# Feature-major attention on 64x64 array tiles, with softmax sums from ones matmuls, in a fused attention and FFN kernel

## The chip, the cores and the metric

The kernel runs on one core of one Trainium2 chip. The metric is device time in microseconds (us), the lower the better.

## The reference, cut to what matters

Linformer attention, then an FFN with a squared relu. There are 8 batches of 8 heads, 1024 tokens and 64 features per head. The keys and values are first projected from 1024 tokens to 64 rows.

```python
k_proj = einsum('ks,bhsd->bhkd', E, k)          # E: 64 x 1024
v_proj = einsum('ks,bhsd->bhkd', F, v)
scores = q @ k_proj.T / sqrt(64)                # per head 1024 x 64
attn   = softmax(scores)
x      = attn @ v_proj                          # heads side by side: 8192 x 512
out    = maximum(x @ w_in, 0)**2 @ w_out        # 512 -> 2048 -> 512
```

All matmuls run in bf16. Per batch the FFN needs 2 x 128 matmuls of 128x128 weights and 512 columns.

## The kernel before

The code is written so that the attention of batch b+1 stands ahead of the FFN of batch b; a scheduler then fills the waits of the one with matmuls of the other. The parts that the change touches:

```python
# per pair of heads: Q transposed, scores on block-diagonal K, softmax
for i in range(NI):
    nc.tensor.transpose(ps_qt[:, i, :], Q_sb[:, i, h0*D:(h0+2)*D], ident_bf[:, :])
nc.vector.tensor_copy(QT_sb[:], ps_qt ...)
for ch in range(2):
    nc.tensor.matmul(ps_sc, lhsT=kprojT_blk[:, pr, :], rhs=QT_sb[:, ch*512:(ch+1)*512], ...)
    nc.scalar.activation(expT_sb[...], ps_sc[:], AF.Exp, scale=SCALE)
# values: tokens on the partitions; two more columns of vprojB give the sums
for (i0, ng) in [(0, 3), (3, 3), (6, 2)]:
    for gi in range(ng):
        nc.tensor.matmul(ps_av[:, gi, :], lhsT=expT_sb[:, i*P:(i+1)*P], rhs=vprojB[:, pr, :], ...)
    nc.vector.reciprocal(recip, ps_av[..., 2*D:2*D+2])
    nc.vector.tensor_tensor(out=x_b..., in0=ps_av..., in1=recip..., op=ALU.mult)
...
# x is token-major, the FFN wants it feature-major: 32 transposes per batch
for cb in range(NCB):
    for i in range(NI):
        nc.tensor.transpose(ps_xt[:, i, :], x_b[:, i, cb*P:(cb+1)*P], ident_bf[:, :])
    nc.scalar.copy(xT_b[:, cb, :], ps_xt ...)
```

The loads stand in this order on one queue: K, V, Q of batch 0, w_in, w_out, then K, V, Q of batch 1 and so on.

The softmax here doesn't subtract the row's maximum and nothing guards it: scores larger than these inputs give would overflow.

## Time and profile before

| | before |
|---|---|
| time, median of 4 runs | 581.15 us (580.04 to 582.84) |
| span of the profiled execution | 577.8 us |
| TensorE (PE) busy | 92% |
| one steady batch | 65.86 us |
| first FFN matmul | 57.81 us |

From the page of the kernel before, the busy time by engine, and the share of the DMA engines' time in 40 slices of 14.4 us (tenths, 9 is 90% or more):

```profile
PE 533.3 (92%) x2998; PEld 259.8 (45%) x3056; DVE 180.9 (31%) x412; ACT 242.9 (42%) x353; POOL 45.7 (8%) x32
DMA  9999999038901792028901694010010101010101
```

TensorE is the bound, and in the first seven slices the DMA engines are busy for 90% or more. The windows view of the kernel before, one batch of the steady part (start:end, length, busy time and instructions of each engine, granted clock, DMA share, GB/s):

```profile
189.50:255.40 65.90, 65.22 (x376) 31.83 (x382) 21.89 (x51) 30.15 (x45) 5.30 (x3) 1.00 0.54 81
```

TensorE is busy for 65.2 of 65.9 us at full clock. What fills a batch is read from the timeline of TensorE in the kernel before (start, length, engine, line, what, count); first the prologue, then a steady batch:

```profile
48.75 0.58 PE L111 MATMUL ps_bank<-K_sb,ET_sb 128*64 128x512 bf16 x1 [5.97 <-DMA K_sb<-in_k_dram]
53.85 0.64 PE L119 MATMUL ps_bank<-V_sb,FT_sb 128*64 128x512 bf16 x1 [4.52 <-DMA V_sb<-in_v_dram]
...
57.81 0.96 PE L229 MATMUL ps_h<-xT_b,w_in_sb 128*128 128x512 bf16 x3 [0.33 <-issue]
...
60.50 0.62 PE L163 MATMUL ps_bank<-ident_bf,Q_sb 128*128 128x128 bf16 x8 [1.50 <-DMA Q_sb<-in_q_dram]
...
190.76 0.38 PE L111 MATMUL ps_bank<-K_sb,ET_sb 128*64 128x512 bf16 x1
190.77 0.38 PE L119 MATMUL ps_bank<-V_sb,FT_sb 128*64 128x512 bf16 x1
191.08 1.04 PE L229 MATMUL ps_h<-xT_b,w_in_sb 128*128 128x512 bf16 x3
...
193.74 0.59 PE L175 MATMUL ps_bank<-QT_sb,kprojT_blk 128*128 128x512 bf16 x2
194.17 1.46 PE L229 MATMUL ps_h<-xT_b,w_in_sb 128*128 128x512 bf16 x6
195.46 0.78 PE L191 MATMUL ps_bank<-vprojB,expT_sb 128*128 128x130 bf16 x8
196.08 0.61 PE L163 MATMUL ps_bank<-ident_bf,Q_sb 128*128 128x128 bf16 x8
196.53 1.67 PE L229 MATMUL ps_h<-xT_b,w_in_sb 128*128 128x512 bf16 x7
...
210.32 3.40 PE L229 MATMUL ps_h<-xT_b,w_in_sb 128*128 128x512 bf16 x15
```

How to read it. A length of a group runs to the end of its last matmul, and one matmul lasts 0.38 us, but they overlap in the pipe. The cost of a matmul is therefore the distance between starts: (3.40 - 0.38) / 14 = 0.216 us for 512 columns. So a batch's 256 FFN matmuls take 55.3 us, and the other 10.6 us of a period are the attention of the next batch. One pair of heads takes 0.43 us for its scores (193.74 to 194.17), 0.62 to 0.73 us for its values (0.62 from 195.46 to 196.08) and 0.45 us for its Q transposes (196.08 to 196.53). The last K and V matmuls of the projection start 0.01 us apart on two 64-column halves of the array and share one slot. Their slot would end at 190.77 + 0.216 = 190.99 us, but the next matmul on the full array starts at 191.08 us: 0.1 us is lost in the change of tiling.

The prologue is another matter. TensorE waits 5.97 us for batch 1's K and 4.52 us for its V, and only then starts its first FFN matmul, at 57.81 us. It is also slower there: the granted clock was 0.62 between 22.0 and 57.8 us, against 1.00 in the steady batch, and the slots of batch 1's projection last 0.43 us, not 0.216.

### The profile page before, as it was taken

What the parts mean: (1) busy time and instruction counts of PE and PEld (TensorE: products, weight loads), DVE (VectorE), ACT (ScalarE), POOL (GpSimd) and SP (SyncE); (2) the same over time, 40 slices, a digit from 0 to 9 for tenths busy, and PEclk for the clock granted to TensorE, in tenths of its full rate; (3) what the DMA queues carried; (4) which work ended last, traced back from release to release, by engine and by line L of the source; (5) the groups of instructions that cost most, each with busy time, mean ns of one, the idle gap of its engine ahead of it and who ended that gap; (6) DMA issues with size and microseconds to landing.
All of it is one profiled execution on the core that took longest, in us unless ns stands there. A gap on an engine that the chain in (4) does not pass through costs nothing.

```text
span 577.8 us, 7241 instructions
## 1 busy us (share of the span) xinstructions
PE 533.3 (92%) x2998; PEld 259.8 (45%) x3056; DVE 180.9 (31%) x412; ACT 242.9 (42%) x353; POOL 45.7 (8%) x32
## 2 busy tenths in 40 slices
PE   0662899999999999999999999999999999999997
PEld 0340454445444454445544454445544454444443
DVE  3350550217121550317221460307312360303030
ACT  0131562436442572526543571526533472515251
POOL 7300320012000120012000120000000000000000
PEclk9865999999999999999999999999999999999999
DMA  9999999038901792028901694010010101010101
GB/s 163 190 207 189 193 192 142 19 76 130 105 36 49 133 110 75 1 77 142 110 36 38 122 115 84 8 74 1 20 54 31 42 2 56 18 56 19 74 0 74
DMA packets 94305, 47.13 MB, mean 82 GB/s; under 512 B 67008, under 2 KB 85440, under 8 KB 94272
## 3 DMA queue, kind: packets, MB, share of 16 engines
q0 software_dynamic: 84896, 29.36, 45.0%
q10 hardware_dynamic: 9376, 17.31, 7.8%
q8 instruction: 24, 0.39, 0.3%
q14 instruction: 9, 0.07, 0.0%
HBM read 59.24 MB, written 16.78 MB: 132 GB/s over the span
## 4 chain that ended last, share of the span: by engine, by line
PE 78%; DMA 6%; DVE 5%; ACT 4%; issue 4%; POOL 2%; ACTq 0%; POOLq 0%
PE ps_bank L246 38%; PE ps_h L229 31%; DMA Q_sb<-in_q_dram 6%; ACT expT_sb L182 3%; PE ps_bank L214 2%; PE ps_bank L191 2%; PE ps_bank L111 2%; PE ps_bank L163 2%; DVE hsqT L239 2%; ACT h_relu L237 1%; DVE x_b L201 1%; DVE QT_sb L169 1%; PE ps_bank L175 1%; DVE recip L199 1%; POOL Q_sb L78 1%
## 5 line engine op out<-in xcount | busy, mean ns | idle before, releaser
L229 PE MATMUL ps_h<-xT_b,w_in_sb 128*128 128x512 bf16 x990 | 231.6, 379 | 1.9 <-issue 0.3
L246 PE MATMUL ps_bank<-w_out_sb,hsqT 128*128 128x512 bf16 x1000 | 222.2, 379 | 1.3
L237 ACT ACTIVATE h_relu<-ps_h 128x1024 bf16<-128x1024 f32 x128 | 130.8, 1031 | 81.0 <-PE ps_h L229 81.0
L239 DVE TENSOR_TENSOR hsqT<-h_relu 128x1024 bf16<-128x1024 bf16 x128 | 88.5, 691 | 232.8 <-ACT h_relu L237 232.8
L246 PEld LDWEIGHTS <-hsqT 128*128 128x128 bf16 x1024 | 100.1, 98 | 120.9
L229 PEld LDWEIGHTS <-w_in_sb 128*128 128x128 bf16 x1024 | 98.0, 98 | 112.1 <-issue 3.8
L254 ACT COPY o_sb<-ps_bank 128x512 f32<-128x512 f32 x64 | 37.5, 587 | 174.6 <-PE ps_bank L246 174.6
L182 ACT ACTIVATE expT_sb<-ps_bank 128x512 bf16<-128x512 f32 x64 | 34.7, 596 | 27.9 <-PE ps_bank L175 27.9
L201 DVE TENSOR_TENSOR x_b<-ps_bank,recip 128x384 bf16<-128x384 f32 (+1 forms) x96 | 44.5, 491 | 0.2
L129 DVE CAST kproj_sb<-ps_bank 64x512 bf16<-64x512 f32 x8 | 5.5, 683 | 102.0 <-PE ps_bank L119 83.5
L78 POOL DMA_DIRECT2D Q_sb<-in_q_dram x8 | 28.5, 3564 | 103.1 <-PE ps_bank L163 46.2
L215 ACT COPY xT_b<-ps_bank 128x1024 bf16<-128x1024 bf16 x32 | 30.8, 1031 | 7.5 <-PE ps_bank L214 7.5
L191 PE MATMUL ps_bank<-vprojB,expT_sb 128*128 128x130 bf16 x256 | 26.4, 230 | 3.4 <-ACT expT_sb L182 1.4
L199 DVE RECIPROCAL recip<-ps_bank 128x6 f32<-128x6 f32 (+1 forms) x96 | 18.1, 189 | 24.5 <-PE ps_bank L191 23.7
L191 PEld LDWEIGHTS <-expT_sb 128*128 128x128 bf16 x256 | 15.8, 101 | 21.1 <-ACT expT_sb L182 20.6
L163 PE MATMUL ps_bank<-ident_bf,Q_sb 128*128 128x128 bf16 x256 | 21.3, 231 | 4.0 <-DMA Q_sb<-in_q_dram 4.0
L68 POOL DMA_DIRECT2D K_sb<-in_k_dram x8 | 9.5, 1188 | 191.0 <-PE ps_bank L119 190.2
L111 PE MATMUL ps_bank<-K_sb,ET_sb 128*64 128x512 bf16 x64 | 19.1, 444 | 6.0 <-DMA K_sb<-in_k_dram 6.0
L175 PE MATMUL ps_bank<-QT_sb,kprojT_blk 128*128 128x512 bf16 x64 | 20.3, 400 | 4.1 <-DVE QT_sb L169 4.1
L119 PE MATMUL ps_bank<-V_sb,FT_sb 128*64 128x512 bf16 x64 | 18.7, 444 | 4.7 <-DMA V_sb<-in_v_dram 4.7
L169 DVE COPY QT_sb<-ps_bank 128x1024 bf16<-128x1024 bf16 x32 | 21.4, 670 | 4.6 <-PE ps_bank L163 4.4
L137 ACT CAST vprojB<-ps_bank 64x64 bf16<-64x64 f32 x32 | 6.7, 209 | 32.4 <-PE ps_bank L119 32.1
(31 smaller groups left out, 116.0 us busy)
## 6 DMA issues: line engine op xcount, KB each, us to landing
out_dram<-o_sb ACTq DMA_DIRECT2D x64, 256.0 KB, 2.0
K_sb<-in_k_dram POOLq DMA_DIRECT2D x8, 1024.0 KB, 9.5
V_sb<-in_v_dram POOLq DMA_DIRECT2D x8, 1024.0 KB, 14.5
Q_sb<-in_q_dram POOLq DMA_DIRECT2D x8, 1024.0 KB, 15.1
w_in_sb<-in_moe_w_in_dram POOLq DMA_DIRECT2D x1, 2048.0 KB, 27.5
w_out_sb<-in_moe_w_out_dram POOLq DMA_DIRECT2D x1, 2048.0 KB, 35.9
e_f_108<-in_E_dram ACTq DMA_DIRECT2D x1, 256.0 KB, 3.5
e_f_122<-in_F_dram ACTq DMA_DIRECT2D x1, 256.0 KB, 7.1
```

Source lines behind the costliest of these rows:

```text
L78: nc.gpsimd.dma_start(Q_sb[:].rearrange("p i (h d) -> p i h d", h=H), q[b].rearrange("h (p i) d -> p i h d", i=NI),)
L111: nc.tensor.matmul(ps_k[0:KP, :], lhsT=ET_sb[:, i, :], rhs=K_view[:, :, i, :], start=(i == 0), stop=(i == NI - 1), tile_position=(0, 0),)
L163: nc.tensor.transpose(ps_qt[:, i, :], Q_sb[:, i, h0 * D:(h0 + 2) * D], ident_bf[:, :],)
L182: nc.scalar.activation(expT_sb[:, ch * CHW:(ch + 1) * CHW], ps_sc[:], AF.Exp, scale=SCALE)
L191: nc.tensor.matmul(ps_av[:, gi, :], lhsT=expT_sb[:, i * P:(i + 1) * P], rhs=vprojB[:, pr, :], start=True, stop=True,)
L201: nc.vector.tensor_tensor(out=out_view.rearrange("p g (h d) -> p g h d", h=2), in0=ps_av[:, 0:ng, 0:2 * D].rearrange("p g (h d) -> p g h d ...
L215: nc.scalar.copy(xT_b[:, cb, :], ps_xt[:].rearrange("p i q -> p (i q)"))
L229: nc.tensor.matmul(ps_h[:, half, :], lhsT=w_in_sb[:, cb, fb * P:(fb + 1) * P], rhs=xT_b[:, cb, ch * TCH:(ch + 1) * TCH], start=(cb == 0), ...
L237: nc.scalar.activation(h_relu[:], ps_h[:].rearrange("p a t -> p (a t)"), AF.Relu)
L239: nc.vector.tensor_tensor(out=hsq_view, in0=h_relu[:], in1=h_relu[:], op=ALU.mult)
L246: nc.tensor.matmul(ps_o[:, :], lhsT=hsqT[:, fb, tb * P:(tb + 1) * P], rhs=w_out_sb[:, fb, :], start=(fb == 0), stop=(fb == NFB - 1),)
L254: nc.scalar.copy(o_sb[:], ps_o[:])
```

## The change

The intent is to take work off TensorE. Attention now works with features on the partitions throughout, so its output is already what the FFN wants, and the 32 x transposes per batch go. The price is that softmax sums can no longer be a column of the values matmul. A matmul of ones with the exponentials puts each token's sum on all 64 partitions of its head. 1/sum is Exp(-Ln(sum)) on ScalarE, and one multiply of 128x1024 on VectorE ends the pair. All score, sum and value matmuls have a contraction of 64 and 64 output rows, so four of them are put on the four 64x64 tiles of the array. Besides, Q is loaded in long runs, as K and V were already, the weights come in four pieces each, relu works on 512 columns instead of 1024, the output is stored from SyncE's queue instead of ScalarE's, and the order of TensorE's instructions is fixed by hand: attention stages of the next batch stand between groups of FFN matmuls.

```diff
-    nc.gpsimd.dma_start(Q_sb..."p i (h d) -> p i h d", q[b]."h (p i) d -> p i h d")
+    nc.gpsimd.dma_start(t[:], q[b].rearrange("h (p i) d -> p h (i d)", i=NI))
...
-            ps_sc <- two matmuls of kprojT_blk (128x128, block-diagonal)
+            for o, bank, h, r, qt in ((lo, 0, h0, lo, q0), (hi, 0, h0, hi, q0),
+                                      (hi, 1, h1, lo, q1), (lo, 1, h1, hi, q1)):
+                nc.tensor.matmul(ps[o, bank, :], lhsT=self.kT[r, h, :], rhs=qt[r], start=True, stop=True)
+            nc.scalar.activation(e[:], ps[:], AF.Exp, scale=SCALE)
...
-            32 values matmuls, reciprocal and multiply by groups, x transposes, copies
+            quads = ((lo, 0, h0, lo, 0), (hi, 0, h1, hi, 1), (hi, 1, h1, lo, 1), (lo, 1, h0, hi, 0))
+            for o, par, h, r, bank in quads:
+                nc.tensor.matmul(ps_s[o, par, :], lhsT=ones[r, :], rhs=e[r, bank, :], ...)
+            for o, par, h, r, bank in quads:
+                nc.tensor.matmul(ps_x[o, par, :], lhsT=self.vp[r, h, :], rhs=e[r, bank, :], ...)
+            nc.scalar.activation(rs[:], ps_s[:], AF.Ln)
+            nc.scalar.activation(rs[:], rs[:], AF.Exp, scale=-1.0)
+            nc.vector.tensor_tensor(out=self.xT[:, pr, :]..., in0=ps_x[:], in1=rs[:], op=ALU.mult)
...
+        def stages(self):           # the number: FFN groups that come before the stage
+            yield self.project, 3
+            yield lambda: self.transpose_q(0), 2
+            yield self.transpose_k, 1
+            for pr in range(NPAIR):
+                yield lambda pr=pr: self.scores(pr), 2
+                if pr + 1 < NPAIR:
+                    yield lambda pr=pr: self.transpose_q(pr + 1), 1
+                yield lambda pr=pr: self.values(pr), 2
...
+    with tc.manual_schedule(engines={PE}):
+        (attention of batch 0 alone, then FFN groups with the stages between)
```

Here lo and hi are partitions 0 to 63 and 64 to 127: o picks the column half of the array (and the output partitions), r its row half. Attention has two PSUM buffers of two banks each, the FFN four of one bank.

More of the change, by code (lines that the diff above doesn't have):

```diff
@@ L13 @@
 ALU = mybir.AluOpType
+PE = mybir.EngineType.PE
 @with_exitstack
@@ L35 @@
     DM = moe_w_out.shape[1]
-    assert D == 64 and KP == 64 and C == CM == 512 and S % 1024 == 0 and H % 2 == 0
+    assert D == 64 and KP == 64 and C == CM == 512 and S == 1024 and H % 2 == 0
     NI = 8
-    assert S == NI * P
     NPAIR = H // 2
@@ L41 @@
     NFB = FF // P
+    NT = NI // 2
+    TCH = NT * P
+    WP = 4
     SCALE = 1.0 / float(D) ** 0.5
@@ L47 @@
     wpool = ctx.enter_context(tc.tile_pool(name="wpool", bufs=1))
+    stage = ctx.enter_context(tc.tile_pool(name="stage", bufs=2))
     qkv_pool = ctx.enter_context(tc.tile_pool(name="qkv", bufs=2))
-    bwork = ctx.enter_context(tc.tile_pool(name="bwork", bufs=2))
-    qt_pool = ctx.enter_context(tc.tile_pool(name="qt_pool", bufs=2))
-    pairpool = ctx.enter_context(tc.tile_pool(name="pairpool", bufs=2))
-    pwork = ctx.enter_context(tc.tile_pool(name="pwork", bufs=2))
-    ffn_sb = ctx.enter_context(tc.tile_pool(name="ffn_sb", bufs=2))
@@ L54 @@
-    out_pool = ctx.enter_context(tc.tile_pool(name="out_pool", bufs=3))
-    aps = ctx.enter_context(tc.tile_pool(name="aps", bufs=4, space=bass.MemoryType.PSUM))
-    fps = ctx.enter_context(tc.tile_pool(name="fps", bufs=2, space=bass.MemoryType.PSUM))
-    def psum_bank(shape, dtype):
-        return aps.tile(shape, dtype, tag="bank", name="ps_bank")
-    ident_bf = const_pool.tile([P, P], BF16, name="ident_bf")
-    w_in_sb = wpool.tile([P, NCB, FF], BF16, name="w_in_sb")
-    w_out_sb = wpool.tile([P, NFB, DM], BF16, name="w_out_sb")
@@ L66, in load_qkv @@
-    def load_qkv(b):
-        K_sb = qkv_pool.tile([P, H, NI * D], BF16, name="K_sb")
-        nc.gpsimd.dma_start(
-            K_sb[:],
-            k[b].rearrange("h (p i) d -> p h (i d)", i=NI),
-        )
-        V_sb = qkv_pool.tile([P, H, NI * D], BF16, name="V_sb")
-        nc.gpsimd.dma_start(
-            V_sb[:],
-            v[b].rearrange("h (p i) d -> p h (i d)", i=NI),
-        )
-        Q_sb = qkv_pool.tile([P, NI, C], BF16, name="Q_sb")
-        nc.gpsimd.dma_start(
-            Q_sb[:].rearrange("p i (h d) -> p i h d", h=H),
-            q[b].rearrange("h (p i) d -> p i h d", i=NI),
-        )
-        return Q_sb, K_sb, V_sb
@@ L84 @@
-    attention_inputs_0 = load_qkv(0)
-    make_identity(nc, ident_bf[:])
-    nc.gpsimd.dma_start(w_in_sb[:], moe_w_in.rearrange("(cb p) f -> p cb f", p=P))
-    nc.gpsimd.dma_start(w_out_sb[:], moe_w_out.rearrange("(fb p) m -> p fb m", p=P))
-    ET_sb = const_pool.tile([P, NI, KP], BF16, name="ET_sb")
-    FT_sb = const_pool.tile([P, NI, KP], BF16, name="FT_sb")
-    with tc.tile_pool(name="stage", bufs=1) as stage_pool:
-        for proj_mat, T_sb in ((E, ET_sb), (F, FT_sb)):
-            e_f32 = stage_pool.tile([KP, S], F32, name="e_f32")
-            nc.scalar.dma_start(e_f32[:], proj_mat[:])
-            e_bf = stage_pool.tile([KP, S], BF16, name="e_bf")
-            nc.vector.tensor_copy(e_bf[:], e_f32[:])
-            ps_et = psum_bank([P, NI, KP], BF16)
-            e_view = e_bf[:].rearrange("k (p i) -> k i p", i=NI)
-            for i in range(NI):
-                nc.tensor.transpose(ps_et[:, i, :], e_view[:, i, :], ident_bf[0:KP, 0:KP])
-            nc.vector.tensor_copy(T_sb[:], ps_et[:])
@@ L103, in attention @@
-    def attention(b, qkv_tiles):
-        Q_sb, K_sb, V_sb = qkv_tiles
-        ps_k = psum_bank([P, C], F32)
-        ps_v = psum_bank([P, C], F32)
-        K_view = K_sb[:].rearrange("p h (i d) -> p h i d", i=NI)
-        V_view = V_sb[:].rearrange("p h (i d) -> p h i d", i=NI)
-        for i in range(NI):
-            nc.tensor.matmul(
-                ps_k[0:KP, :],
-                lhsT=ET_sb[:, i, :],
-                rhs=K_view[:, :, i, :],
-                start=(i == 0),
-                stop=(i == NI - 1),
-                tile_position=(0, 0),
-            )
-            nc.tensor.matmul(
-                ps_v[KP:2 * KP, :],
-                lhsT=FT_sb[:, i, :],
-                rhs=V_view[:, :, i, :],
-                start=(i == 0),
-                stop=(i == NI - 1),
-                tile_position=(0, KP),
-            )
-        kproj_sb = bwork.tile([KP, H, D], BF16, name="kproj_sb")
-        nc.vector.tensor_copy(
-            kproj_sb[:].rearrange("k h d -> k (h d)"), ps_k[0:KP, :]
-        )
-        vprojB = bwork.tile([P, NPAIR, 2 * D + 2], BF16, name="vprojB")
-        nc.vector.memset(vprojB[:], 0.0)
-        for pr in range(NPAIR):
-            h0 = 2 * pr
-            h1 = h0 + 1
-            nc.scalar.copy(vprojB[0:KP, pr, 0:D], ps_v[KP:2 * KP, h0 * D:(h0 + 1) * D])
-            nc.scalar.copy(
-                vprojB[KP:2 * KP, pr, D:2 * D], ps_v[KP:2 * KP, h1 * D:(h1 + 1) * D]
-            )
-        nc.vector.memset(vprojB[0:KP, :, 2 * D:2 * D + 1], 1.0)
-        nc.vector.memset(vprojB[KP:2 * KP, :, 2 * D + 1:2 * D + 2], 1.0)
-        ps_kpT = psum_bank([P, NPAIR, KP], BF16)
-        for pr in range(NPAIR):
-            h0 = 2 * pr
-            nc.tensor.transpose(
-                ps_kpT[:, pr, :],
-                kproj_sb[0:KP, h0:h0 + 2, :],
-                ident_bf[0:KP, 0:KP],
-            )
-        kprojT_blk = bwork.tile([P, NPAIR, 2 * KP], BF16, name="kprojT_blk")
-        nc.vector.memset(kprojT_blk[:], 0.0)
-        nc.vector.tensor_copy(kprojT_blk[0:D, :, 0:KP], ps_kpT[0:D, :, :])
-        nc.vector.tensor_copy(kprojT_blk[D:2 * D, :, KP:2 * KP], ps_kpT[D:2 * D, :, :])
-        x_b = pwork.tile([P, NI, C], BF16, name="x_b")
-        for pr in range(NPAIR):
-            h0 = 2 * pr
-            ps_qt = psum_bank([P, NI, P], BF16)
-            for i in range(NI):
-                nc.tensor.transpose(
-                    ps_qt[:, i, :],
-                    Q_sb[:, i, h0 * D:(h0 + 2) * D],
-                    ident_bf[:, :],
-                )
-            QT_sb = qt_pool.tile([P, NI * P], BF16, name="QT_sb")
-            nc.vector.tensor_copy(QT_sb[:], ps_qt[:].rearrange("p i q -> p (i q)"))
-            expT_sb = pairpool.tile([P, NI * P], BF16, name="expT_sb")
-            NCH = 2
-            CHW = (NI * P) // NCH
-            for ch in range(NCH):
-                ps_sc = psum_bank([P, CHW], F32)
-                nc.tensor.matmul(
-                    ps_sc[:, :],
-                    lhsT=kprojT_blk[:, pr, :],
-                    rhs=QT_sb[:, ch * CHW:(ch + 1) * CHW],
-                    start=True,
-                    stop=True,
-                )
-                nc.scalar.activation(
-                    expT_sb[:, ch * CHW:(ch + 1) * CHW], ps_sc[:], AF.Exp, scale=SCALE
-                )
-            groups = [(0, 3), (3, 3), (6, 2)]
-            for (i0, ng) in groups:
-                ps_av = psum_bank([P, 3, 2 * D + 2], F32)
-                for gi in range(ng):
-                    i = i0 + gi
-                    nc.tensor.matmul(
-                        ps_av[:, gi, :],
-                        lhsT=expT_sb[:, i * P:(i + 1) * P],
-                        rhs=vprojB[:, pr, :],
-                        start=True,
-                        stop=True,
-                    )
-                recip = pairpool.tile([P, 3, 2], F32, name="recip")
-                nc.vector.reciprocal(recip[:, 0:ng, :], ps_av[:, 0:ng, 2 * D:2 * D + 2])
-                out_view = x_b[:, i0:i0 + ng, h0 * D:(h0 + 2) * D]
-                nc.vector.tensor_tensor(
-                    out=out_view.rearrange("p g (h d) -> p g h d", h=2),
-                    in0=ps_av[:, 0:ng, 0:2 * D].rearrange("p g (h d) -> p g h d", h=2),
-                    in1=recip[:, 0:ng, :].rearrange("p g (h o) -> p g h o", o=1).to_broadcast(
-                        [P, ng, 2, D]
-                    ),
-                    op=ALU.mult,
-                )
-        xT_b = pwork.tile([P, NCB, NI * P], BF16, name="xT_b")
-        for cb in range(NCB):
-            ps_xt = psum_bank([P, NI, P], BF16)
-            for i in range(NI):
-                nc.tensor.transpose(ps_xt[:, i, :], x_b[:, i, cb * P:(cb + 1) * P], ident_bf[:, :])
-            nc.scalar.copy(xT_b[:, cb, :], ps_xt[:].rearrange("p i q -> p (i q)"))
-        return xT_b
@@ L218, in ffn @@
-    def ffn(b, xT_b):
-        NCHUNK = 2
-        TCH = (NI * P) // NCHUNK
-        IPC = NI // NCHUNK
-        for ch in range(NCHUNK):
-            hsqT = ffn_sb.tile([P, NFB, TCH], BF16, name="hsqT")
-            for fb2 in range(NFB // 2):
-                ps_h = fps.tile([P, 2, TCH], F32, name="ps_h")
-                for half in range(2):
-                    fb = 2 * fb2 + half
-                    for cb in range(NCB):
-                        nc.tensor.matmul(
-                            ps_h[:, half, :],
-                            lhsT=w_in_sb[:, cb, fb * P:(fb + 1) * P],
-                            rhs=xT_b[:, cb, ch * TCH:(ch + 1) * TCH],
-                            start=(cb == 0),
-                            stop=(cb == NCB - 1),
-                        )
-                h_relu = ffn_sb.tile([P, 2 * TCH], BF16, name="h_relu")
-                nc.scalar.activation(h_relu[:], ps_h[:].rearrange("p a t -> p (a t)"), AF.Relu)
-                hsq_view = hsqT[:, 2 * fb2:2 * fb2 + 2, :].rearrange("p a t -> p (a t)")
-                nc.vector.tensor_tensor(
-                    out=hsq_view, in0=h_relu[:], in1=h_relu[:], op=ALU.mult
-                )
-            for tb in range(IPC):
-                i = ch * IPC + tb
-                ps_o = psum_bank([P, DM], F32)
-                for fb in range(NFB):
-                    nc.tensor.matmul(
-                        ps_o[:, :],
-                        lhsT=hsqT[:, fb, tb * P:(tb + 1) * P],
-                        rhs=w_out_sb[:, fb, :],
-                        start=(fb == 0),
-                        stop=(fb == NFB - 1),
-                    )
-                o_sb = out_pool.tile([P, DM], F32, name="o_sb")
-                nc.scalar.copy(o_sb[:], ps_o[:])
-                nc.scalar.dma_start(out_rows[b, i, :, :], o_sb[:])
@@ L257 @@
-    qkv_next = attention_inputs_0
-    xT_cur = attention(0, qkv_next)
-    for b in range(B):
-        if b + 1 < B:
-            qkv_t = load_qkv(b + 1)
-            xT_next = attention(b + 1, qkv_t)
-        else:
-            xT_next = None
-        ffn(b, xT_cur)
-        xT_cur = xT_next
+    proj_pool = ctx.enter_context(tc.tile_pool(name="proj", bufs=2))
+    qt_pool = ctx.enter_context(tc.tile_pool(name="qt", bufs=2))
+    soft_pool = ctx.enter_context(tc.tile_pool(name="soft", bufs=3))
@@ new lines, with att_psum @@
+    x_pool = ctx.enter_context(tc.tile_pool(name="x", bufs=2))
+    relu_pool = ctx.enter_context(tc.tile_pool(name="relu", bufs=8))
+    hsq_pool = ctx.enter_context(tc.tile_pool(name="hsq", bufs=2))
+    out_pool = ctx.enter_context(tc.tile_pool(name="outp", bufs=4))
+    aps = ctx.enter_context(tc.tile_pool(name="aps", bufs=2, space=bass.MemoryType.PSUM))
+    fps = ctx.enter_context(tc.tile_pool(name="fps", bufs=4, space=bass.MemoryType.PSUM))
+    def att_psum(shape, dtype):
+        return aps.tile(shape, dtype, tag="att", name="ps_att")
@@ new lines, in ffn_psum, with load @@
+    def ffn_psum():
+        return fps.tile([P, 512], F32, tag="ffn", name="ps_ffn")
+    def load(b):
+        tiles = []
+        for name, src in (("K_sb", k), ("V_sb", v), ("Q_sb", q)):
+            t = qkv_pool.tile([P, H, NI * D], BF16, name=name)
+            nc.gpsimd.dma_start(t[:], src[b].rearrange("h (p i) d -> p h (i d)", i=NI))
+            tiles.append(t)
+        return tiles
+    e_f32 = []
+    for src in (E, F):
+        t = stage.tile([KP, S], F32, name="e_f32")
+        nc.sync.dma_start(t[:], src[:])
+        e_f32.append(t)
@@ new lines @@
+    kvq = load(0)
+    nc.scalar.preload_act_table_set("natural_log_exp_and_others")
+    ident = const_pool.tile([P, P], BF16, name="ident")
+    make_identity(nc, ident[:])
+    ones = const_pool.tile([P, D], BF16, name="ones")
+    nc.vector.memset(ones[:], 1.0)
+    w_in_view = moe_w_in.rearrange("(cb p) f -> p cb f", p=P)
+    w_out_view = moe_w_out.rearrange("(fb p) m -> p fb m", p=P)
+    w_in_sb, w_out_sb = [], []
+    fw = FF // WP
+    for j in range(WP):
+        t = wpool.tile([P, NCB, fw], BF16, name=f"w_in_{j}")
+        nc.gpsimd.dma_start(t[:], w_in_view[:, :, j * fw:(j + 1) * fw])
+        w_in_sb.append(t)
@@ new lines, with w_in_blk, w_out_blk @@
+    for j in range(WP):
+        n = NFB // WP
+        t = wpool.tile([P, n, DM], BF16, name=f"w_out_{j}")
+        nc.gpsimd.dma_start(t[:], w_out_view[:, j * n:(j + 1) * n, :])
+        w_out_sb.append(t)
+    def w_in_blk(cb, fb):
+        n = fw // P
+        return w_in_sb[fb // n][:, cb, (fb % n) * P:(fb % n + 1) * P]
+    def w_out_blk(fb):
+        n = NFB // WP
+        return w_out_sb[fb // n][:, fb % n, :]
+    projT = []
+    for n, src in zip(("ET", "FT"), e_f32):
+        e_bf = stage.tile([KP, S], BF16, name="e_bf")
+        nc.vector.tensor_copy(e_bf[:], src[:])
+        ps = att_psum([P, NI, KP], BF16)
+        view = e_bf[:].rearrange("k (p i) -> k i p", i=NI)
+        for i in range(NI):
+            nc.tensor.transpose(ps[:, i, :], view[:, i, :], ident[0:KP, 0:KP])
+        t = const_pool.tile([P, NI, KP], BF16, name=n)
+        nc.vector.tensor_copy(t[:], ps[:])
+        projT.append(t)
@@ new lines, with __init__, project, transpose_k @@
+    ET, FT = projT
+    class Attention:
+        def __init__(self, b, kvq):
+            self.K, self.V, self.Q = kvq
+            self.xT = x_pool.tile([P, NCB, 2 * TCH], BF16, name="xT")
+            self.exp, self.ps_x = {}, {}
+        def project(self):
+            ps = att_psum([P, C], F32)
+            kv = self.K[:].rearrange("p h (i d) -> p h i d", i=NI)
+            vv = self.V[:].rearrange("p h (i d) -> p h i d", i=NI)
+            for i in range(NI):
+                f, l = i == 0, i == NI - 1
+                nc.tensor.matmul(ps[0:KP, :], lhsT=ET[:, i, :], rhs=kv[:, :, i, :], start=f, stop=l)
+                nc.tensor.matmul(ps[KP:P, :], lhsT=FT[:, i, :], rhs=vv[:, :, i, :], start=f, stop=l)
+            self.kp = proj_pool.tile([KP, H, 2, D], BF16, name="kp")
+            ps_k = ps[0:KP, :].rearrange("k (h d) -> k h d", h=H)
+            nc.vector.tensor_copy(self.kp[:, :, 0, :], ps_k)
+            nc.vector.tensor_copy(self.kp[:, :, 1, :], ps_k)
+            self.vp = proj_pool.tile([P, H, D], BF16, name="vp")
+            ps_v = ps[KP:P, :].rearrange("k (h d) -> k h d", h=H)
+            nc.scalar.copy(self.vp[KP:P], ps_v)
+            nc.scalar.copy(self.vp[0:KP], ps_v)
+        def transpose_k(self):
+            ps = att_psum([P, H, KP], BF16)
+            for h in range(H):
+                nc.tensor.transpose(
+                    ps[:, h, :], self.kp[:, h].rearrange("k a d -> k (a d)"), ident[0:KP, 0:KP]
+                )
+            self.kT = proj_pool.tile([P, H, KP], BF16, name="kT")
+            nc.vector.tensor_copy(self.kT[:], ps[:])
+        def transpose_q(self, pr):
+            ps = att_psum([P, 2, TCH], BF16)
+            for a in range(2):
+                for n in range(NT):
+                    nc.tensor.transpose(
+                        ps[:, a, n * P:(n + 1) * P], self.Q[:, 2 * pr + a, n * P:(n + 1) * P], ident[:]
+                    )
+            t = qt_pool.tile([P, 2, TCH], BF16, name="qT")
+            nc.vector.tensor_copy(t[:], ps[:])
+            self.qt = getattr(self, "qt", {})
+            self.qt[pr] = t
+        def qT(self, h):
+            return self.qt[h // 2][:, h % 2, :]
+        def scores(self, pr):
+            h0, h1 = 2 * pr, 2 * pr + 1
+            ps = att_psum([P, 2, TCH], F32)
+            lo, hi = slice(0, 64), slice(64, 128)
+            q0, q1 = self.qT(h0), self.qT(h1)
+            for o, bank, h, r, qt in ((lo, 0, h0, lo, q0), (hi, 0, h0, hi, q0),
+                                      (hi, 1, h1, lo, q1), (lo, 1, h1, hi, q1)):
+                nc.tensor.matmul(ps[o, bank, :], lhsT=self.kT[r, h, :], rhs=qt[r], start=True, stop=True)
+            e = soft_pool.tile([P, 2, TCH], BF16, name="expT")
+            nc.scalar.activation(e[:], ps[:], AF.Exp, scale=SCALE)
+            self.exp[pr] = e
+        def values(self, pr):
+            h0, h1 = 2 * pr, 2 * pr + 1
+            e = self.exp.pop(pr)
+            lo, hi = slice(0, 64), slice(64, 128)
+            quads = ((lo, 0, h0, lo, 0), (hi, 0, h1, hi, 1), (hi, 1, h1, lo, 1), (lo, 1, h0, hi, 0))
+            ps_s = att_psum([P, 2, TCH], F32)
+            for o, par, h, r, bank in quads:
+                nc.tensor.matmul(ps_s[o, par, :], lhsT=ones[r, :], rhs=e[r, bank, :], start=True, stop=True)
+            ps_x = att_psum([P, 2, TCH], F32)
+            for o, par, h, r, bank in quads:
+                nc.tensor.matmul(ps_x[o, par, :], lhsT=self.vp[r, h, :], rhs=e[r, bank, :], start=True, stop=True)
+            rs = soft_pool.tile([P, 2, TCH], F32, name="rs")
+            nc.scalar.activation(rs[:], ps_s[:], AF.Ln)
+            nc.scalar.activation(rs[:], rs[:], AF.Exp, scale=-1.0)
+            nc.vector.tensor_tensor(
+                out=self.xT[:, pr, :].rearrange("p (a t) -> p a t", a=2), in0=ps_x[:], in1=rs[:], op=ALU.mult
+            )
+        def stages(self):
[7 more added lines that the diff above has]
+                yield lambda pr=pr: self.values(pr), 2
@@ new lines, in ffn_groups, with first, second @@
+    def ffn_groups(b, xT):
+        groups = []
+        def first(ch, hsq, fb):
+            ps = ffn_psum()
+            for cb in range(NCB):
+                nc.tensor.matmul(
+                    ps[:], lhsT=w_in_blk(cb, fb), rhs=xT[:, cb, ch * TCH:(ch + 1) * TCH],
+                    start=(cb == 0), stop=(cb == NCB - 1),
+                )
+            r = relu_pool.tile([P, TCH], BF16, name="h_relu")
+            nc.scalar.activation(r[:], ps[:], AF.Relu)
+            nc.vector.tensor_tensor(out=hsq[:, fb, :], in0=r[:], in1=r[:], op=ALU.mult)
+        def second(ch, hsq, tb):
+            ps = ffn_psum()
+            for fb in range(NFB):
+                nc.tensor.matmul(
+                    ps[:], lhsT=hsq[:, fb, tb * P:(tb + 1) * P], rhs=w_out_blk(fb),
+                    start=(fb == 0), stop=(fb == NFB - 1),
+                )
+            o = out_pool.tile([P, DM], F32, name="o_sb")
+            nc.scalar.copy(o[:], ps[:])
+            nc.sync.dma_start(out_rows[b, 2 * tb + ch, :, :], o[:])
+        for ch in range(2):
+            hsq = hsq_pool.tile([P, NFB, TCH], BF16, name="hsq")
+            for fb in range(NFB):
+                groups.append(lambda ch=ch, hsq=hsq, fb=fb: first(ch, hsq, fb))
+            for tb in range(NT):
+                groups.append(lambda ch=ch, hsq=hsq, tb=tb: second(ch, hsq, tb))
+        return groups
@@ new lines @@
+    with tc.manual_schedule(engines={PE}):
+        cur = Attention(0, kvq)
+        for stage_fn, _ in cur.stages():
+            stage_fn()
+        for b in range(B):
+            nxt = Attention(b + 1, load(b + 1)) if b + 1 < B else None
+            pending = list(nxt.stages()) if nxt else []
+            wait = pending[0][1] if pending else 0
+            for g in ffn_groups(b, cur.xT):
+                g()
+                wait -= 1
+                while pending and wait <= 0:
+                    pending.pop(0)[0]()
+                    wait = pending[0][1] if pending else 0
+            for stage_fn, _ in pending:
+                stage_fn()
+            cur = nxt
```

## The prediction

> **What bounds the kernel now.** TensorE. The busy table gives PE 92% of a 577.8 us span against ACT 42% and DVE 31%; the chain of waits is 78% PE. FFN matmuls start every 0.216 us, so a batch's 256 take 55.2 us. Batches repeat every 65.86 us (windows view: 65.8 to 65.9), PE busy throughout, clock 1.00. So attention costs TensorE about 10.65 us per batch (timeline, steady batch): K/V projection 1.95, K transposes 0.3, Q transposes 1.8, scores 1.73, values 2.8, x transposes 1.8. In the prologue the first FFN matmul starts at 57.8 us, after waits on DMA (K 6.0, V 4.7, Q 4.0 us in the list of waits); batch 1's Q lands at 60.5 us.
>
> **What changes on TensorE, per steady batch.**
> - x transposes vanish: -1.8 us.
> - Scores: per head pair four 64x64-tile matmuls instead of two full ones. If the four overlap, 0.22 us instead of 0.43. The projection already runs two column tiles in one 0.216 us slot. The Trainium skill, "TensorE: Matmul & The Clock Gate", Part 3, reports row and column tiles composing nearly ideally; no run here shows four yet.
> - Values: 32 matmuls at about 0.08 to 0.09 us become two rounds of four per pair: 0.43 us instead of 0.7.
> - Switches: the skill's "TensorEngine Tiling (Array Packing)", Key Properties, says that changing the tiling mode drains TensorE. The trace agrees: about 0.1 us is lost on either side of the projection. Eight new tiled blocks per batch add some 0.2 us each, 1.6 us.
> - K transposes double: +0.2 us.
>
> New attention: 1.95+0.5+1.8+1.8 (scores)+2.7 (values) = 8.75 us, saving 1.9 us.
>
> **What moves off TensorE.** ACT gets Ln and Exp(-1) of 128x1024 per pair (1.03 us each, as the Relu of that size) and relu in halves (0.596 each), but loses the xT copies; some 37 of 65 us. DVE loses reciprocals and small multiplies, gains a 128x1024 multiply, about 1.15 us. Neither should bind on average. But PE order is now fixed and attention has only two PSUM buffers: the third Q transpose of a batch must wait for Ln, Exp and multiply of the first pair (over 3.2 us plus queued relus) with about 3.1 us of PE work planned between. I expect 0.5 us of PE stall per batch. Net gain 1.4 us per batch, times 7 = 10 us.
>
> **Prologue.** Q in long runs should load like K (5.1 us instead of 6.65). The first attention alone gets slower (a chain of about 6 us per pair instead of 4.3), so the first FFN matmul comes at about 49 us; ten more FFN matmuls run before batch 1's Q arrives at 57. Gain about 6 us.
>
> **Prediction:** 566 us, 80% range 554 to 577. Faster by over 2% 0.65, within 2% 0.27, slower by over 2% 0.08.
>
> **What would show it right.** Period near 64.4 us per batch; groups of four tiled matmuls starting together every 0.22 us; first FFN matmul near 49 us; no transposes of x; list of waits showing PE waiting for DVE (xT multiply) or ACT (Ln) under 1 us per batch.
>
> **What would make it wrong.** If only two tiles overlap, attention grows by 2.6 us per batch and the steady gain is gone (about 585 us). If switches or 64-column weight loads cost 0.4 us per block, half the gain goes. If the fixed order stalls on ACT in every pair (Ln/Exp queued behind relus), 2 us per batch are lost.

## The result, and the profile after

| | before | after |
|---|---|---|
| time, median of 4 runs each | 581.15 us | 565.74 us (565.24 to 565.79) |
| ratio | | 0.9735, 95% interval 0.971 to 0.976 |
| span of the profiled execution | 577.8 us | 563.9 us |
| one steady batch | 65.86 us | 64.42 us |
| first FFN matmul that does not wait again | 57.81 us | 43.95 us |
| first Q transpose of batch 1 | 60.50 us | 59.39 us |

The ratio, here and below, is the mean time of a kernel's fast runs over that of the fast runs of the kernel before from the same rounds, so it is not quite the ratio of the medians. The profiled execution of the kernel before was one of its shorter ones, so the spans differ by 13.9 us where the medians differ by 15.4 us.

The page after, busy time by engine:

```profile
PE 522.4 (93%) x2841; PEld 232.1 (41%) x2896; DVE 178.8 (32%) x349; ACT 284.0 (50%) x433; POOL 28.4 (5%) x38
```

The windows view after, one steady batch:

```profile
186.57:250.99 64.42, 63.52 (x354) 28.20 (x362) 21.89 (x43) 35.09 (x54) 2.63 (x3) 1.00 0.41 82
```

From the list of TensorE's waits after (who waited for whom: us in total, times, the longest):

```profile
PE ps_att L141 <- DMA V_sb<-in_v_dram: 8.9, 2, 4.5
...
PE ps_ffn L227 <- issue: 2.6, 15, 0.3
PE ps_att L165 <- DVE xT L205: 2.2, 7, 0.3
PE ps_ffn L227 <- DVE xT L205: 1.7, 1, 1.7
```

And the timeline of TensorE after, prologue and a steady batch:

```profile
28.41 0.64 PE L185 MATMUL ps_att<-qT,kT 64*64 64x512 bf16 x4 [0.50 <-ACT rs L203]
30.41 1.01 PE L165 MATMUL ps_att<-ident,Q_sb 128*128 128x128 bf16 x8 [1.36 <-ACT expT L187]
...
33.12 0.64 PE L185 MATMUL ps_att<-qT,kT 64*64 64x512 bf16 x4 [0.28 <-ACT rs L203]
...
43.95 4.00 PE L227 MATMUL ps_ffn<-xT,w_in_112 128*128 128x512 bf16 x9 [1.65 <-DVE xT L205]
47.93 0.64 PE L140 MATMUL ps_att<-K_sb,ET 128*64 128x512 bf16 x1
53.04 0.58 PE L141 MATMUL ps_att<-V_sb,FT 128*64 128x512 bf16 x1 [4.48 <-DMA V_sb<-in_v_dram]
...
59.39 0.61 PE L165 MATMUL ps_att<-ident,Q_sb 128*128 128x128 bf16 x8
...
193.48 1.89 PE L227 MATMUL ps_ffn<-xT,w_in_116 128*128 128x512 bf16 x8
195.30 0.41 PE L198 MATMUL ps_att<-expT,ones 64*64 64x512 bf16 x4
195.54 0.39 PE L201 MATMUL ps_att<-expT,vp 64*64 64x512 bf16 x4
195.85 1.04 PE L227 MATMUL ps_ffn<-xT,w_in_116 128*128 128x512 bf16 x4
...
199.37 0.61 PE L165 MATMUL ps_att<-ident,Q_sb 128*128 128x128 bf16 x8 [0.31 <-DVE xT L205]
```

What to see. First, four 64x64 matmuls of 512 columns are one row with a length of 0.41 us, and the next four start 0.24 us after them (195.30 to 195.54). All four do run at once: a full-array matmul alone takes 0.216 us. Second, the change of tiling has its price. The eight FFN matmuls from 193.48 us would be done with their slots at 193.48 + 8 x 0.216 = 195.21 us and the FFN goes on at 195.85 us, so sums and values took 0.64 us, of which 2 x 0.216 are matmul slots and 0.21 us is the way into the 64x64 mode and out. Third, the one wait in the steady part is the third Q transpose of each batch, 0.31 us for the multiply of the first pair, once in each of seven batches; that multiply had itself waited for Ln and Exp on ScalarE. (The 15 waits for "issue" are places where a matmul's record is missing: the list of e1_free_order, whose 2896 records are complete, has none.) Fourth, the FFN starts far earlier than before and then runs into batch 1's V: 4.48 us of nothing, at a point where w_in is there and FFN matmuls are left. So batch 1's first Q transpose comes only 1.1 us earlier than before, although 20 FFN matmuls stand in front of it, where there were 4 (one of them is missing in the records; so is one of the first 12 after). The clock is low here too, 0.62 between 43.95 and 58.2 us: the FFN matmuls from 43.95 us start (4.00 - 0.64) / 8 = 0.42 us apart.

The gain by parts, from the traces: seven steady batches at 65.86 - 64.42 = 1.44 us make 10.1 us. At batch 1's first Q transpose the new kernel is 60.50 - 59.39 = 1.1 us ahead and has 16 more FFN matmuls behind it (16 x 0.216 = 3.5 us), less some 0.4 us of K transposes that it still has to do: 4.2 us. Together 14.3 us, against 13.9 us in the spans.

### The profile page after: what moved, and what is told of

Its sections match the earlier page's. It is cut to its first block, busy times and chain, and to the rows that moved or that the text cites. A ratio compares the mean times of both kernels' runs of the same rounds, so it can differ in the third digit from the quotient of the medians.

```text
span 563.9 us, 7122 instructions
## 1 busy us (share of the span) xinstructions
PE 522.4 (93%) x2841; PEld 232.1 (41%) x2896; DVE 178.8 (32%) x349; ACT 284.0 (50%) x433; POOL 28.4 (5%) x38
## 4 chain that ended last, share of the span: by engine, by line
PE 79%; DMA 8%; ACT 7%; DVE 4%; issue 1%; POOL 1%; ACTq 0%; POOLq 0%
PE ps_ffn L238 39%; PE ps_ffn L227 32%; DMA V_sb<-in_v_dram 4%; DMA w_in_114<-in_moe_w_in_dram 4%; DVE xT L205 3%; ACT rs L204 3%; PE ps_att L165 2%; ACT rs L203 2%; PE ps_att L140 2%; ACT h_relu L232 1%; PE ps_att L198 1%; PE ps_att L185 1%; DVE hsq L233 1%; PE ps_att L141 1%; PE ps_att L201 1%
## 5 line engine op out<-in xcount | busy, mean ns | idle before, releaser
L232 ACT ACTIVATE h_relu<-ps_ffn 128x512 bf16<-128x512 f32 x256 | 147.4, 597 | 73.1 <-PE ps_ffn L227 73.0
L233 DVE TENSOR_TENSOR hsq<-h_relu 128x512 bf16<-128x512 bf16 x256 | 105.4, 423 | 216.2 <-ACT h_relu L232 215.7
L238 PEld LDWEIGHTS <-hsq 128*128 128x128 bf16 x1024 | 98.8, 98 | 120.3 <-issue 4.5
L243 ACT COPY o_sb<-ps_ffn 128x512 f32<-128x512 f32 x64 | 37.5, 586 | 173.7 <-PE ps_ffn L238 173.7
L227 PE MATMUL ps_ffn<-xT,w_in_112 128*128 128x512 bf16 x255 | 64.7, 394 | 2.0 <-DVE xT L205 1.7
L238 PE MATMUL ps_ffn<-w_out_124,hsq 128*128 128x512 bf16 x255 | 65.6, 379 | 0.1
L238 PE MATMUL ps_ffn<-w_out_120,hsq 128*128 128x512 bf16 x255 | 65.6, 380 | 0.0
L238 PE MATMUL ps_ffn<-w_out_122,hsq 128*128 128x512 bf16 x248 | 65.1, 379 | 0.4
L238 PE MATMUL ps_ffn<-w_out_126,hsq 128*128 128x512 bf16 x235 | 62.3, 379 | 1.1
L227 PE MATMUL ps_ffn<-xT,w_in_114 128*128 128x512 bf16 x241 | 59.7, 381 | 1.5 <-issue 1.1
L227 PE MATMUL ps_ffn<-xT,w_in_116 128*128 128x512 bf16 x256 | 60.3, 380 | 0.0
L227 PE MATMUL ps_ffn<-xT,w_in_118 128*128 128x512 bf16 x248 | 58.6, 379 | 1.2 <-issue 1.1
L205 DVE TENSOR_TENSOR xT<-ps_att,rs 128x1024 bf16<-128x1024 f32 x32 | 39.2, 1225 | 53.0 <-ACT rs L204 53.0
L227 PEld LDWEIGHTS <-w_in_112 128*128 128x128 bf16 x256 | 23.8, 100 | 37.1 <-issue 13.5
L227 PEld LDWEIGHTS <-w_in_118 128*128 128x128 bf16 x256 | 24.2, 98 | 28.5 <-issue 1.6
L227 PEld LDWEIGHTS <-w_in_116 128*128 128x128 bf16 x256 | 23.6, 98 | 29.8 <-issue 4.5
L227 PEld LDWEIGHTS <-w_in_114 128*128 128x128 bf16 x256 | 23.8, 98 | 29.0 <-issue 3.9
L203 ACT ACTIVATE rs<-ps_att 128x1024 f32<-128x1024 f32 x32 | 32.9, 1027 | 4.9 <-PE ps_att L198 4.9
L204 ACT ACTIVATE rs<-rs 128x1024 f32<-128x1024 f32 x32 | 33.8, 1056 | 1.0
```

The lines of the kernel that those rows point to most:

```text
L203: nc.scalar.activation(rs[:], ps_s[:], AF.Ln)
L204: nc.scalar.activation(rs[:], rs[:], AF.Exp, scale=-1.0)
L205: nc.vector.tensor_tensor(out=self.xT[:, pr, :].rearrange("p (a t) -> p a t", a=2), in0=ps_x[:], in1=rs[:], op=ALU.mult)
L227: nc.tensor.matmul(ps[:], lhsT=w_in_blk(cb, fb), rhs=xT[:, cb, ch * TCH:(ch + 1) * TCH], start=(cb == 0), stop=(cb == NCB - 1),)
L232: nc.scalar.activation(r[:], ps[:], AF.Relu)
L233: nc.vector.tensor_tensor(out=hsq[:, fb, :], in0=r[:], in1=r[:], op=ALU.mult)
```

## The experiments

Besides the changed kernel, seven variants were run, all with correct results.

| run | time (median) | ratio to the kernel before | steady batch |
|---|---|---|---|
| after | 565.74 us | 0.9735 | 64.42 us |
| e1_free_order | 565.57 us | 0.9739 | 64.42 us |
| e2_split_values | 572.36 us | 0.9854 | 65.38 us |
| e3_full_array | 570.78 us | 0.983 | 64.79 us |
| e4_late_wout | 557.83 us | 0.9607 | 64.42 us |
| e5_recip | 698.71 us (one run, state unknown) | | |
| e6_before_late_wout | 571.58 us | 0.9839 | 65.86 us |
| e7_combined | 554.07 us | 0.9537 | 64.12 us |

The steady batch is half the distance between the same VectorE instruction two batches apart.

The theory was that the gain is the TensorE work as counted (x transposes gone, packing partly eaten by changes of tiling) and, in the prologue, an earlier FFN. The rivals were that the fixed order makes the gain, that the packing alone makes it, and that the prologue's share has nothing to do with attention but with the loads.

### e1_free_order: is it the fixed order?

```diff
-    with tc.manual_schedule(engines={PE}):
+    if True:
```

> The changed kernel without the fixed TensorE order. The two TensorE programs were compared before the run: from the second batch on they are the same, only the first attention is interleaved otherwise. Theory (the gain is in the matmul work and in the way the stages are written down, not in the fixing of the order): 564.7 to 566.7 us, period 64.4 us per batch. Rival (the fixed order is what removes stalls): above 570 us.

It took 565.57 us, the same as the changed kernel. Fixing the order gives nothing here: the stages are written between the FFN groups, and the scheduler keeps them there by itself. As the two TensorE programs are the same from the second batch on, this run tells nothing of what another order, or a coarser way of writing the stages, would cost. In the prologue the order does differ: only 4 FFN matmuls, not 12, run before batch 1's K and V, and yet the time is the same. Why is not shown: between 57.5 and 62.0 us the granted clock was 1.00 in this run and 0.85 in the changed kernel, which makes up for a part.

### e2_split_values: what does a visit to the 64x64 mode cost?

```diff
 def values(self, pr):
     (four sums matmuls, Ln, Exp)
+def values_x(self, pr):                  # a stage of its own, one FFN group later
     (four values matmuls, multiply)
-                yield lambda pr=pr: self.scores(pr), 2
+                yield lambda pr=pr: self.scores(pr), (2 if pr == 0 else 1)
+                yield lambda pr=pr: self.values_x(pr), 1      # after values
```

> The sums matmuls and the values matmuls of a pair are parted by one FFN group, so that there is one more change of tiling mode in and one more out per pair, 4 pairs a batch. Theory (a visit to the 64x64 mode costs 0.2 to 0.22 us besides its matmuls): period longer by 0.8 to 0.9 us, 65.2 to 65.3 us, and 571 to 573 us in all. Rival (mode changes are nearly free, what is paid in a block is its matmuls and weight loads): below 567.5 us.

It took 572.36 us. The timeline of TensorE in this run:

```profile
197.16 0.41 PE L198 MATMUL ps_att<-expT,ones 64*64 64x512 bf16 x4
197.50 1.04 PE L232 MATMUL ps_ffn<-xT,w_in 128*128 128x512 bf16 x4
198.47 0.41 PE L208 MATMUL ps_att<-expT,vp 64*64 64x512 bf16 x4
198.81 1.04 PE L232 MATMUL ps_ffn<-xT,w_in 128*128 128x512 bf16 x4
```

The four FFN matmuls from 197.50 us would end their slots at 198.36 us, the tiled ones start at 198.47 us, and the FFN goes on at 198.81 us: 0.11 us into the mode, and 0.34 - 0.216 = 0.12 us beyond the slot on the way out. The period grew by 0.95 us. The third Q transpose now waited 0.42 us instead of 0.31, so 0.84 us are left for four more visits, 0.21 us each. The theory held, with a period slightly longer than the 65.2 to 65.3 us expected. The rival, that mode changes are nearly free, is out. The Trainium skill, "TensorEngine Tiling (Array Packing)", Key Properties, says that a change of tiling mode drains TensorE. The 0.21 us are what a visit costs here, but how much of it is the drain is not shown: the first weight loads of a visit also start only with its matmuls (195.29 us for matmuls at 195.30 us in the changed kernel), where on the full array they run ahead (198.44 us for 198.66 us in e3_full_array), and no run separates the two.

### e3_full_array: feature-major without packing

```diff
-  four matmuls on 64x64 tiles for scores, four for sums, four for values
+  two matmuls each on block-diagonal 128x128 weights:
+    matmul(ps[:, a, :],   lhsT=self.kT[:, pr, :], rhs=self.qt[pr][:, a, :])
+    matmul(ps_s[:, a, :], lhsT=ones[:],           rhs=e[:, a, :])
+    matmul(ps_x[:, a, :], lhsT=self.vp[:, pr, :], rhs=e[:, a, :])
+  (kT, vp and ones zero off the diagonal; 4 K transposes instead of 8;
+   Q loaded in short runs and token order of the output as in the kernel before)
```

> Feature-major attention kept (ones matmuls, exp(-ln), no x transposes, the same order of stages), but on full 128x128 block-diagonal weights instead of 64x64 tiles: 2+2+2 matmuls of 512 columns per pair instead of three rounds of four tiled ones, no mode change around them, K transposes halved, Q loaded in short runs as before. Theory (feature-major is most of the steady gain, packing only a little, as the mode changes eat most of it): 1.29 us per pair instead of 1.08, less 0.3 us for K, so period 64.8 to 65.1 us, and with a prologue 1.5 us longer through the Q load 569 to 573 us. Rival (the packing is the gain): period at or above 65.8 us and 576 us or more.

It took 570.78 us, with a period of 64.79 us. The timeline of TensorE in this run:

```profile
195.19 0.59 PE L187 MATMUL ps_att<-qT,kT 128*128 128x512 bf16 x2
195.62 1.03 PE L226 MATMUL ps_ffn<-xT,w_in 128*128 128x512 bf16 x4
...
198.66 0.60 PE L197 MATMUL ps_att<-expT,ones 128*128 128x512 bf16 x2
199.09 0.59 PE L200 MATMUL ps_att<-expT,vp 128*128 128x512 bf16 x2
199.52 1.89 PE L226 MATMUL ps_ffn<-xT,w_in 128*128 128x512 bf16 x8
...
201.68 1.03 PE L226 MATMUL ps_ffn<-xT,w_in 128*128 128x512 bf16 x4
202.83 0.61 PE L171 MATMUL ps_att<-ident,Q_sb 128*128 128x128 bf16 x8
```

And the place of these last two lines in e1_free_order, which has the steady batch of the changed kernel and all its records:

```profile
198.05 1.04 PE L227 MATMUL ps_ffn<-xT,w_in 128*128 128x512 bf16 x4
199.40 0.61 PE L165 MATMUL ps_att<-ident,Q_sb 128*128 128x128 bf16 x8 [0.31 <-DVE xT L205]
```

Scores take 0.43 us, sums and values 0.86 us, and the FFN follows without a gap. So 65.86 - 64.79 = 1.07 us of the 1.44 us per batch come without any 64x64 tile, and 0.37 us from the packing. The theory held; the rival, 576 us or more, is out. That the 1.07 us come from the feature-major form, and not from the other edits, is seen when the distances between starts are summed over a steady batch (e6_before_late_wout below has that of the kernel before, with all records): the x transposes, 1.79 us, are gone, sums and values take 3.46 instead of 2.79 us, and the FFN with all gaps before and within it 55.75 instead of 55.69 us. Nothing is left for relu in halves or weights in pieces.

For the scores packing gives nothing: one visit with one round of four takes 0.216 + 0.22 = 0.44 us, the two full matmuls 0.43 us. It pays in the values block, where two rounds share a visit: 0.64 us instead of 0.86. Packing spares 12 slots per batch, 12 x 0.216 = 2.59 us. The same sums in e1_free_order show where most of it goes: eight visits take 1.93 us (0.23 us each at the scores, 0.25 at sums and values, with the gap between the two rounds), the doubled K transposes 0.12 us, and the third Q transpose 0.18 us. It waits for the multiply in both kernels, but by starts it loses 1.15 - 0.86 = 0.29 us here (201.68 to 202.83) and 1.35 - 0.88 = 0.47 us with the tiles (198.05 to 199.40). That leaves 0.36 us.

The rest of the difference in time, 5.04 - 7 x 0.37 = 2.5 us, lies in the prologue, where this run waits for batch 1's V until 55.56 us and for its Q until 62.25 us. Its Q loads have the short runs of the kernel before.

### e4_late_wout: is the prologue bound by the order of the loads?

```diff
     (loads of w_in)
+    kvq1 = load(1)
     (loads of w_out)
-            nxt = Attention(b + 1, load(b + 1)) if b + 1 < B else None
+            nxt = Attention(b + 1, load(b + 1) if b else kvq1) if b + 1 < B else None
```

> The loads of batch 1 are issued before those of w_out. Theory (the prologue is bound by the order of the loads: batch 1's V lands at 53 us behind w_out, which is not needed before about 66 us): V of batch 1 lands near 43 us, TensorE no longer waits 4.5 us for it, time to batch 1's first Q transpose 59.4 to about 52 us, in all 557 to 560 us with the period unchanged at 64.4 us. Rival (the first attention or the clock binds the prologue, or w_out now comes too late): above 563 us.

It took 557.83 us, 7.9 us less than the changed kernel, with an unchanged period. The timeline of TensorE in this run:

```profile
43.34 4.00 PE L228 MATMUL ps_ffn<-xT,w_in 128*128 128x512 bf16 x9 [1.65 <-DVE xT L206]
47.27 0.64 PE L141 MATMUL ps_att<-K_sb,ET 128*64 128x512 bf16 x1
47.27 0.63 PE L142 MATMUL ps_att<-V_sb,FT 128*64 128x512 bf16 x1
...
51.51 0.61 PE L166 MATMUL ps_att<-ident,Q_sb 128*128 128x128 bf16 x8
```

The wait for batch 1's V is gone, and its first Q transpose comes at 51.51 us instead of 59.39. The load queue had been serving w_out, first used at 65.47 us in this run, ahead of what TensorE stood waiting for.

### e5_recip: why Exp(-Ln) and not a reciprocal?

```diff
-            nc.scalar.activation(rs[:], ps_s[:], AF.Ln)
-            nc.scalar.activation(rs[:], rs[:], AF.Exp, scale=-1.0)
+            nc.vector.reciprocal(rs[:], ps_s[:])
```

> The changed kernel with one VectorE reciprocal of 128x1024 in place of Ln and Exp on ScalarE. Of the kernel before, a reciprocal of 128x6 took 196 ns and one of 128x4 174 ns, 11 ns for each further element. Theory (that slope holds, so the exp(-ln) is what makes feature-major normalisation affordable): about 11 us for one, 45 us of VectorE per batch, TensorE stalls behind it in every pair, 620 us or more. Rival (the slope of such small ones says nothing, it runs at the pace of the 128x1024 multiply, 1.23 us): 562 to 568 us.

One run gave 698.71 us. The groups of instructions in this run (busy us, mean ns of one, idle before), the reciprocal and for comparison the multiply of the same size:

```profile
L203 DVE RECIPROCAL rs<-ps_att 128x1024 f32<-128x1024 f32 x32 | 209.8, 6557 | 38.5 <-PE ps_att L198 37.6
L204 DVE TENSOR_TENSOR xT<-ps_att,rs 128x1024 bf16<-128x1024 f32 x32 | 38.8, 1213 | 0.4
```

The reciprocal takes 6.56 us where the multiply takes 1.21 us. TensorE waited 82 us in all for it, and 24 us more for the FFN's squares, which VectorE makes too. That the time would be 620 us or more was expected; the size of one reciprocal was not: 6.4 ns per element, not the 11 ns read off the tiny ones of the kernel before. A slope between two operations of a few elements is a poor guide to a large one. The two activations of the changed kernel, whose place it takes, need 1.03 and 1.06 us. The Trainium skill, "VectorE: DVE Perf Modes", First, the fixed hardware budget, describes the reciprocal as an iterative divide with a repeat count of 8; that it takes 5.4 times as long as the multiply fits this, but no run here shows the iterations.

### e6_before_late_wout: the same edit in the old kernel

```diff
     nc.gpsimd.dma_start(w_in_sb[:], ...)
+    attention_inputs_1 = load_qkv(1)
     nc.gpsimd.dma_start(w_out_sb[:], ...)
-            qkv_t = load_qkv(b + 1)
+            qkv_t = load_qkv(b + 1) if b else attention_inputs_1
```

> The kernel before, with the loads of batch 1 issued before that of w_out and nothing else changed. Theory (the prologue of both kernels is bound by the order of the loads, so this alone gives the old kernel about what the whole rewriting gave): batch 1's Q, on which the first steady period waits at 60.5 us, lands at about 50.5 us; period still 65.86 us; 569 to 573 us. Rival (in the kernel before the first attention alone, not the loads, held the FFN back): above 576 us.

It took 571.58 us, inside the 569 to 573 us of the theory; the rival is out. The timeline of TensorE in this run:

```profile
50.38 1.03 PE L164 MATMUL ps_bank<-ident_bf,Q_sb 128*128 128x128 bf16 x8 [3.53 <-DMA Q_sb<-in_q_dram]
51.21 1.91 PE L230 MATMUL ps_h<-xT_b,w_in_sb 128*128 128x512 bf16 x4
```

Batch 1's Q transposes start at 50.38 us instead of 60.50. Two moved lines give the old kernel 9.4 us of time (580.94 to 571.58 us), where the whole rewriting gave 15.4 us. The two gains overlap in part: the rewriting is worth 571.58 - 557.83 = 13.8 us on top of the late w_out, of which 10.1 us are the seven steady batches.

### e7_combined: the version that the experiments point to

On top of e4_late_wout:

```diff
+  first attention only: the sums go to two of the FFN's PSUM banks, Ln in halves,
+  the three later Q transposes right after the first scores, scores(pr+1) ahead of values(pr)
-                    yield lambda pr=pr: self.transpose_q(pr + 1), 1
-                yield lambda pr=pr: self.values(pr), 2
+                    yield lambda pr=pr: self.transpose_q(pr + 1), 1 + late    # late = int(pr == 1)
+                yield lambda pr=pr: self.values(pr), 2 - late
```

> Late w_out, and two more edits: the sums of the first attention go to the FFN's PSUM banks, idle by then, so that its pairs overlap (its ScalarE chain of 3.1 us a pair should bind in place of 4.7 us a pair); and the third Q transpose of a batch comes one FFN group later (it waited 0.31 us for the multiply). Theory: first FFN matmul that does not wait 2.5 to 3.5 us earlier, period 64.1 us, in all 552 to 555 us. Rival (the loads bind again, now that of batch 1's V and Q; the shifted transpose stalls the values instead): 556.5 to 558.5 us, as with late w_out alone.

It took 554.07 us, the fastest of all, and inside the 552 to 555 us expected. The timeline of TensorE in this run:

```profile
42.00 4.00 PE L249 MATMUL ps_ffn<-xT,w_in 128*128 128x512 bf16 x9 [0.99 <-DVE xT L214]
...
61.94 0.61 PE L166 MATMUL ps_att<-ident,Q_sb 128*128 128x128 bf16 x8
```

The second line is the third Q transpose of batch 1, the one that was shifted. It no longer waits, and the period fell by 0.30 us to 64.12 us, as expected. It does not fall by the whole 0.47 us, as the values matmuls that follow now start 0.38 us after the sums and not 0.24 us. The prologue gained 43.34 - 42.00 = 1.3 us where 2.5 to 3.5 us had been expected. The timeline of ScalarE in this run:

```profile
29.54 1.02 ACT L188 ACTIVATE expT<-ps_att 128x1024 bf16<-128x1024 f32 x1 [2.54 <-PE ps_att L186]
...
37.57 0.60 ACT L210 ACTIVATE rs<-ps_ffn 128x512 f32<-128x512 f32 x1 [0.17 <-PE ps_ffn L203]
```

ScalarE stood still for 2.54 us before the exponential of the second pair, whose scores stood behind three Q transposes and started at 28.85 us. From 29.54 us to the end of its last Exp(-1) at 40.69 us it then had no gap longer than 0.17 us. So the ScalarE chain did become the bound, as the theory said, but it started late, and the 2.54 us would more than make up what is missing. That scores ahead of those transposes would gain it was not tried.

## Why the prediction was right, point by point

The predicted 566 us met 565.74 us. That the total was met so closely is partly luck: the steady batches came out as predicted, the prologue did not. The predicted gains of 10 and 6 us make 16 us; the traces show 10.1 and about 4.2 us, and the medians differ by 15.4 us (the profiled execution of the kernel before was one of its shorter ones, so the traces see less).

| term, per steady batch | predicted | measured |
|---|---|---|
| scores, 4 pairs | 1.8 us | 4 x 0.44 = 1.76 us |
| sums and values, 4 pairs | 2.7 us | 0.64 us for one without a wait; 2.69 us for all four (e1_free_order) |
| visit to the 64x64 mode, each | 0.2 us | 0.21 us |
| TensorE's wait in the fixed order | 0.5 us | 0.31 us as listed, 0.47 us by starts |
| ScalarE busy | 37 us | 35.1 us |
| period | 64.4 us | 64.42 us |
| prologue, gain | 6 us | about 4.2 us |

- That TensorE bounds the kernel and that work taken off it comes back held: the period fell by 1.44 us. ScalarE's busy time per batch rose from 30.15 to 35.09 us, and it held TensorE up in the steady part only through the third Q transpose, which waits for a multiply that waits for Ln and Exp.
- That four 64x64 tiles run at once held (0.24 us for four). The Trainium skill, "TensorE: Matmul & The Clock Gate", Part 3, says that matmuls on different tiles run concurrently in the same array; this trace agrees for the four 64x64 tiles.
- That the switches eat much of the packing held, and e3_full_array shows how much: of the 2.59 us of slots that packing spares per batch, 0.37 us are left in the period.
- One Ln and one Exp per pair cost no reloading of tables. The Trainium skill, "ScalarE: Activation LUTs", Table sets, says that one set holds both functions; the trace has a single table load of 1.28 us.
- The step that failed is the prologue. The first attention was put at 6 us per pair and took 4.71 us (28.41 to 33.12 us). The prediction does not reckon out its 6 us, but in the steady batch it had the third Q transpose wait for the multiply of the first pair, and there it does. In the prologue the same transpose waited for the exponential of the second pair (1.36 us): it started at 30.41 us, while the multiply ran until 30.71 us. It seems to have been given the buffer of the scores, which the exponential reads; that was not tried by itself. The FFN therefore began at 43.95 us, not 49 us. But the step "ten more FFN matmuls run before batch 1's Q arrives" named the wrong load: the FFN ran 12 matmuls and then stood 4.48 us for batch 1's V, which came at 53.04 us, only 0.8 us sooner than before. Long runs did make batch 0's Q faster (5.05 us from V's arrival to Q's, against 6.69 us), as predicted. Yet w_in, w_out and the next K and V together then took 30.5 us, against 30.0 us before. The two errors, an FFN too early by 5 us and a load overlooked, partly cancelled, and that is luck: about 4.2 us were gained, not 6.
- What the prediction did not see at all is that the order of the loads was worth about 8 us in this kernel and 9 us in the old one, more than the packing.

## What to carry to other kernels

Count the visits to a tiling mode as well as the matmuls in it: here a visit costs as much as one full 512-column matmul, so tiles pay where two rounds share a visit and not where one round stands alone. When TensorE is full in the steady part, look at the prologue for what its first wait is for, and load first what is waited for first; two moved lines gave over half of what the rewriting gave. A sum that comes out by a ones matmul, with Exp(-Ln) for its reciprocal, turns an awkward layout into one that needs no transposes, as long as ScalarE has the time.

## What the Trainium skill lacked or had wrong

- "TensorEngine Tiling (Array Packing)", Key Properties, says that a change of tiling mode drains TensorE, but gives no cost. Here a visit costs 0.21 us, about 0.1 us each way (e2_split_values), as much as a 512-column matmul on the full array. Its table of speedups ("Both dimensions") leaves this out, and for one round of four tiles nothing of the speedup is left (0.44 us against 0.43 us).
- "TensorE: Matmul & The Clock Gate", Part 3, has no number for four 64x64 tiles. Here four of 512 columns take one slot of 0.24 us.
- "ScalarE: Activation LUTs", What it computes, says, for accuracy, to use VectorE's reciprocal in place of ScalarE's, and says nothing of its time or of Exp(-Ln). For a 128x1024 tile in PSUM it took 6.56 us (e5_recip), against 1.03 + 1.06 us for Ln and Exp(-1) on ScalarE; their errors were not compared. The reciprocal's time per element, 6.4 ns here (6557 ns over 1024), was found on no page.
